# Adding the last stage's products to an output that stays in memory, by transfers that GpSimd issues

## The chip, the core and the metric

The kernel runs on one core of a Trainium2 chip. A core has five engines with instruction queues of their own: TensorE (PE in the profile; PEld are its weight loads) multiplies matrices into PSUM; VectorE (DVE), ScalarE (ACT) and GpSimd (POOL) do arithmetic; SyncE (SP) mostly issues transfers. ScalarE and GpSimd issue transfers too. All transfers run on 16 DMA engines. SBUF is the on-chip memory of 128 partitions, PSUM holds the products of TensorE, and HBM is the memory outside. In what follows, "memory" is HBM.

The metric is the device time of one execution in microseconds (us).

## What is computed

The input `u` has 2048 positions of 512 channels. Two branches are mixed by a gate, one number per position:

```python
g = sigmoid((x * gate_w).sum(-1, keepdims=True))
a = A(x)      # a long convolution per channel (state space kernel K), by FFT, plus u * Dskip
b = gelu(x @ w1 + b1) @ w2 + b2
return g * a + (1 - g) * b
```

with the convolution as

```python
K = einsum("dn,dnl,dn->dl", Cc, exp(logdA * l), dB).real
y = irfft(rfft(pad(u)) * rfft(pad(K)))[:L] + u * Dskip
```

The output is 2048 by 512 in 32-bit floats, 4 MB.

## The kernel before

The program has two parts. `front` (a list of tasks whose order a planner in the code works out from costs and due times) computes the dense branch `b`, the taps `K`, and the first stages of the Fourier transforms of signal and taps; intermediate results go to memory (`tu_d` for the signal, `tk_d` for the taps). The dense branch's result, already multiplied by `1 - g`, goes to the output tensor `out` in memory: a first half of the hidden units is stored plainly (L974), and the second half is added to it in memory by transfers that GpSimd issues with `accum_op=ALU.add` (L980), 256 KB each. Two of the 16 output tiles of the second half are left over and computed late (`late`, `rest`).

`out` is laid out as 16 tiles of 128 rows by 512 channels, and the last part handles them in eight pairs, k or m from 0 to 7; a pair is two tiles.

`conv` is the last part, and its order is written out by hand. A loop over s from 0 to 15 does, for two frequency groups at a time: `product(s)`, six VectorE instructions that multiply spectra; `signal(s + 1)` and `taps(s + 2)`, second transform stages on TensorE (L1109), whose inputs are loaded ahead by SP (L1090 from `tk_d`, and from `tu_d`); `inverse(s)`, the first stage of the inverse transform on TensorE (L1148); and `turn(s)`, in which ScalarE copies the result to SBUF (L1154) and SP stores it to `t4_d` in memory (L1156), two stores of 256 KB per step. After every eight tiles (a group) the stored rows are loaded back in another arrangement into `den` and `t3` by four transfers of 512 KB (L1164): for the first three groups GpSimd issues them, for the last one ScalarE.

In the steps from s = 8 on, `dense(s - 8)` comes last: it picks a place `mos[k]` in `attic` or `loft` (SBUF space that held the signal's transform) and SP loads pair k of `out` there (L1176), 512 KB. So pair 7's load stands in SP's queue behind the last store to `t4_d`.

After the loop `rest` finishes the two late dense tiles, four matmuls into a tile named `warm` follow (L1225; nobody reads the result), and VectorE adds the late tiles into pair 7 (L1228). Then comes the last stage, a loop over the pairs m: eight matmul instructions give two tiles in PSUM (L1236), and each is multiplied by the gate and added to the loaded dense tile. For ten of the sixteen tiles VectorE does both in one instruction (L1248). For the six in `ASIDE` ScalarE multiplies into a buffer (L1245) and GpSimd adds that (L1246). SP then stores the pair (L1252); the two tiles of pair 7 are stored singly, by SP and ScalarE (L1250).

Of the kernel before, what the change touches and what calls it, by code (L numbers as in the profile page):

```python
# [13 lines left out]
ALU = mybir.AluOpType  # L14
# [61 lines left out]
N_US = N_DEN + N_ROOM  # L76
W_DVE = ((1, 0), (3, 0), (5, 0))

ASIDE = (1, 3, 6, 8, 11, 13)
GROUP = 8  # L80

PI = float(np.pi)
# [193 lines left out]
def gated_mix(  # L276
# [18 lines left out]
    nc = tc.nc  # L295
# [778 lines left out]
    def conv(pool, ps, late, attic, loft, den):  # L1074


        sas = [pool.tile([P, D], F32, name=f"sa{k}", bufs=1) for k in range(6)]
# [5 lines left out]
        def fetch(n):  # L1083
            if n % 4 == 0:
                m = n // 4
                cc = pool.tile([P, 384], F32, tag="cc", name=f"cc{m}", bufs=4)
                nc.sync.dma_start(cc, c2[m])
                c4s[m] = cc
            t2s[n] = pool.tile([P, D], F32, tag="tk", name=f"tk{n}", bufs=N_TK)
            nc.sync.dma_start(t2s[n], tk_d[ko[n]])  # L1090

        def matrices(m):

            cc = c4s[m]
            f = cc[:, 0:256].rearrange("p (n k) -> p n k", n=4)
            f1 = pool.tile([P, 4, 64], F32, tag="f1", name=f"f1{m}", bufs=2)
            nc.scalar.mul(f1[0:64], f[64:128], -1.0)
            nc.scalar.copy(f1[64:128], f[0:64])
            mats[m] = (f, f1), cc[:, 256:384].rearrange("p (s k) -> p s k", s=2)
# [11 lines left out]
        def taps(s):  # L1111
            fac[s] = []
            for c in range(2):
                pk = ps.tile([P, D], F32, tag="pk", name=f"p2k{s}{c}", bufs=2)
                pair(s, 1, c, pk)
                k = pool.tile([P, D], F32, tag=f"k{c}", name=f"k{s}{c}", bufs=2)
                nc.scalar.copy(k, pk)  # L1117
                fac[s].append(k)

        def signal(s):  # L1120
            pus[s] = []
            for c in range(2):
                pu = ps.tile([P, D], F32, tag="pu", name=f"p2u{s}{c}", bufs=4)
                pair(s, 0, c, pu)
                pus[s].append(pu)

        def product(s):

            (ur, ui), (kr, ki) = pus.pop(s), fac.pop(s)
            v = [pool.tile([P, D], F32, tag=f"v{i}", name=f"v{s}{i}", bufs=2) for i in range(2)]  # L1130
            nc.vector.tensor_mul(v[0], ur, kr)
            nc.vector.tensor_mul(v[1], ur, ki)
            nc.vector.tensor_mul(zs[0], ui, ki)
            nc.vector.tensor_mul(zs[1], ui, kr)
            nc.vector.tensor_sub(v[0], v[0], zs[0])
            nc.vector.tensor_add(v[1], v[1], zs[1])
            prod[s] = v

        def inverse(s):

            v = prod.pop(s)
            for i in range(2):
                n = 2 * s + i
                pas[n] = ps.tile([P, D], F32, tag="pa", name=f"pa{s}{i}", bufs=2)
                r = slice(64 * i, 64 * i + 64)
                w = mats[n // 4][1][r, s % 2]
                for c in range(2):
                    nc.tensor.matmul(pas[n][64 * c : 64 * c + 64], w, v[c][r], start=True, stop=True)  # L1148

        def turn(s):  # L1150

            for n in (2 * s, 2 * s + 1):
                sa = sas[n % 6]
                nc.scalar.copy(sa, pas.pop(n))  # L1154
                g, k = divmod(n, GROUP)
                nc.sync.dma_start(t4_d[g, :, k].rearrange("e c q d -> (c q) e d"), sa)  # L1156
                if k < GROUP - 1:
                    continue
                rows = t4_d[g].rearrange("e k c q d -> (e k c) q d")

                for h in range(0, 32, 8):
                    on = nc.gpsimd if n < 31 else nc.scalar
                    to = t3[g:P:4, h - 8 : h] if h else den[g:P:4]
                    on.dma_start(to, rows[:, h : h + 8])  # L1164

        accs, mos = {}, {}

        def dense(k):

            r = 5 + 2 * k if k < 7 else 0  # L1170
            if r < N_ATTIC:
                mos[k] = attic[:, r : r + 2]
            else:
                r -= N_ATTIC
                mos[k] = loft[:, r * D : (r + 2) * D].rearrange("p (s d) -> p s d", s=2)
            nc.sync.dma_start(mos[k], out[2 * k : 2 * k + 2].rearrange("s p d -> p s d"))  # L1176

        def rest(n):

            while late and n:  # L1180
                s, h, l, w, wl = late.pop(0)
                first = s not in accs
                last = not any(e[0] == s for e in late)
                if first:
                    accs[s] = ps.tile([P, D], F32, tag="pk", name=f"acc{s}", bufs=2)
                ss = slice(s * P, (s + 1) * P)
                nc.tensor.matmul(accs[s], h[:, ss], w, start=first, stop=False)
                nc.tensor.matmul(accs[s], h[:, ss], wl, start=False, stop=False)
                nc.tensor.matmul(accs[s], l[:, ss], w, start=False, stop=last)
                n -= 1  # L1190
# [11 lines left out]
        for s in range(16):  # L1202

            for n in range(2 * s + N_TK + (2 if s else 0), min(2 * s + N_TK + 4, 32)):
                fetch(n)
            for n in range(2 * s + N_ROOM, min(2 * s + N_ROOM + 2, 32)) if s > 3 else ():
                nc.sync.dma_start(us[n], tu_d[ko[n]])
            product(s)
            if s + 1 < 16:
                signal(s + 1)  # L1210
            if s + 2 < 16:
                if s % 2 == 0:
                    matrices(s // 2 + 1)
                taps(s + 2)
            if s == 15:
                rest(N_REST)
            inverse(s)
            turn(s)
            if s >= 8:
                dense(s - 8)  # L1220
        rest(14)

        warm = ps.tile([P, D], F32, tag="pa", name="warm", bufs=2)
# [2 lines left out]
        for s in range(N_LATE):  # L1226
            z = mos[7][:, s]
            nc.vector.scalar_tensor_tensor(z, accs[s], gate[:, 1, 14 + s : 15 + s], z, ALU.mult, ALU.add)  # L1228

        for m in range(8):  # L1230
            tag, n = ("pa", 2) if m % 3 == 2 else ("pu", 4)
            pbs = [ps.tile([P, D], F32, tag=tag, name=f"pb{m}{i}", bufs=n) for i in range(2)]
            for i in range(2):
                for b in range(2):
                    j = 4 * m + 2 * i + b
                    nc.tensor.matmul(  # L1236
                        pbs[i][64 * b : 64 * b + 64], g1t[:, min(j, 1)], t3[:, j - 8] if j > 7 else den[:, j],
                        start=True, stop=True,
                    )
            for i in range(2):  # L1240
                t = 2 * m + i
                z, g = mos[m][:, i], gate[:, 0, t : t + 1]
                if t in ASIDE:
                    a = sas[ASIDE.index(t)]
                    nc.scalar.mul(a, pbs[i], g)  # L1245
                    nc.gpsimd.tensor_add(z, z, a)  # L1246
                else:
                    nc.vector.scalar_tensor_tensor(z, pbs[i], g, z, ALU.mult, ALU.add)  # L1248
                if m == 7:
                    (nc.sync, nc.scalar)[i].dma_start(out[t], z)  # L1250
            if m < 7:
                nc.sync.dma_start(out[2 * m : 2 * m + 2].rearrange("s p d -> p s d"), mos[m])  # L1252

    ctx.enter_context(tc.manual_schedule())
    keep = ctx.enter_context(tc.tile_pool(name="keep", bufs=1))
# [8 lines left out]
    with (  # L1264
        tc.tile_pool(name="fp", bufs=2, reuse_waits="tile") as fp,
        tc.tile_pool(name="ps_f", bufs=2, space=PSUM, reuse_waits="tile") as ps_f,
    ):
        conv(fp, ps_f, late, attic, loft, den)
# [64 lines left out]
```

## Time and profile before

| | us |
|---|---|
| three runs: median, lowest, highest | 539.2, 537.0, 542.56 |
| the profiled execution: time | 537.5 |
| the profiled execution: span from first to last event | 535.7 |
| `front` gives way to `conv` | about 425 |
| the last store to `t4_d` is issued | 502.7 |
| the first matmul of the last stage starts | 515.1 |
| the last matmul of the last stage ends | 530.1 |

The page of the profile gives for each engine its busy time and, in a strip of 40 slices, when it was busy; for the DMA engines the mean busy share and the rate in GB/s. The chain that ended last is followed back from the last instruction, at each step to what released it. A row of the timeline gives the start, the busy time, the engine, the line, the operation, the names of what it writes and reads, and how often it came in a row; in brackets stands the idle time before it and what ended that.

### The profile page before, as it was taken

The page shows a single profiled execution, that of the slowest core. Times are in us where ns is not written, and L with a number is a line of the kernel's source. Part 1 is how long each engine was busy: PE and PEld are TensorE (multiplying, and loading weights), DVE is VectorE, ACT ScalarE, POOL GpSimd, SP SyncE. Part 2 cuts the span into 40 slices and gives each one's busy share as a digit, 9 for nine tenths or more (in the row PEclk, how much of TensorE's full clock was granted, in tenths as well). Part 3 has the DMA queues.
Part 4 walks back from the last instruction along what each step waited for, and adds up shares of the span by engine and source line. Part 5 has one row for each costly group of instructions (what it writes and reads, how often), then busy time and mean ns, then how long its engine had stood idle before and what let it go on. Part 6 is the DMA issues. An engine that isn't in the chain of part 4 may idle for free.

```text
span 535.7 us, 12218 instructions
## 1 busy us (share of the span) xinstructions
PE 513.4 (96%) x4818; PEld 387.3 (72%) x4818; DVE 426.3 (80%) x806; ACT 353.5 (66%) x614; POOL 41.3 (8%) x79
## 2 busy tenths in 40 slices
PE   7969999999999999989999999999999999999985
PEld 6637788898899889876988988889888622222621
DVE  5798899999999959869999999999701287777233
ACT  4979956699875599966586988376342555655211
POOL 2000000000000000000112010101010101010123
PEclk9779999999999999999999999999999999999999
DMA  8989674153585442583878037705778858999976
GB/s 260 347 287 308 196 253 138 41 199 90 133 233 171 158 123 78 167 268 76 212 173 258 2 88 145 162 6 133 233 185 181 239 184 272 368 406 373 356 292 260
DMA packets 82469, 107.87 MB, mean 201 GB/s; under 512 B 39318, under 2 KB 43546, under 8 KB 81900
## 3 DMA queue, kind: packets, MB, share of 16 engines
q1 hardware_dynamic: 77020, 86.09, 50.2%
q0 software_dynamic: 5056, 18.65, 13.2%
q10 hardware_dynamic: 336, 2.36, 1.2%
q8 instruction: 38, 0.62, 0.5%
q14 instruction: 19, 0.16, 0.1%
HBM read 61.46 MB, written 45.62 MB: 200 GB/s over the span
## 4 chain that ended last, share of the span: by engine, by line
PE 74%; DMA 11%; ACT 9%; DVE 2%; issue 2%; SPq 0%; ACTq 0%; DVEq 0%
PE pk L682 10%; PE ph L900 8%; PE acc L948 8%; PE ph L902 8%; PE ph L901 8%; PE acc L950 7%; PE acc L949 7%; PE p2u L1109 6%; PE p2k L1109 5%; PE pa L1148 3%; PE pb L1236 3%; DMA attic<-in_xs_dram 2%; DMA tu_d<-attic 2%; PE ph L404 2%; DMA t_d<-sa 2%
## 5 line engine op out<-in xcount | busy, mean ns | idle before, releaser
L900 PE MATMUL ph<-xh,wh 128*128 128x256 f32 x448 | 129.2, 288 | 4.2 <-ACT attic L422 2.3
L902 PE MATMUL ph<-xh,wl 128*128 128x256 f32 x448 | 128.2, 286 | 0.5 <-DVE wl L783 0.4
L901 PE MATMUL ph<-xlo,wh 128*128 128x256 f32 x448 | 127.8, 285 | 0.0
L900 PEld LDWEIGHTS ph<-xh,wh 128*128 128x128 f32 x448 | 86.2, 192 | 14.7 <-issue 5.6
L948 PE MATMUL acc<-wh,hh 128*128 128x512 f32 x210 | 85.5, 407 | 3.0 <-ACT hh L920 3.0
L901 PEld LDWEIGHTS ph<-xlo,wh 128*128 128x128 f32 x448 | 86.3, 193 | 2.0
L902 PEld LDWEIGHTS ph<-xh,wl 128*128 128x128 f32 x448 | 86.4, 193 | 1.2 <-DVE wl L783 1.2
L950 PE MATMUL acc<-wh,hl 128*128 128x512 f32 x210 | 83.3, 396 | 0.4 <-DVE hl L930 0.4
L949 PE MATMUL acc<-wl,hh 128*128 128x512 f32 x210 | 83.2, 396 | 0.0
L917 ACT ACTIVATE ph<-ph,b1t 128x256 f32<-128x256 f32 x112 | 50.4, 450 | 43.1 <-PE ph L902 41.1
L930 DVE TENSOR_TENSOR hl<-ph,hh 128x512 fp32r<-128x512 f32 (+1 forms) x62 | 38.2, 617 | 31.8 <-ACT hh L920 31.5
L682 PE MATMUL pk<-y,den 128*32 128x64 f32 x2048 | 61.4, 290 | 0.0
L682 PEld LDWEIGHTS pk<-y,den 128*32 128x32 f32 x2048 | 57.2, 136 | 3.7 <-issue 1.4
L948 PEld LDWEIGHTS acc<-wh,hh 128*128 128x128 f32 x210 | 40.0, 191 | 18.0 <-issue 6.8
L950 PEld LDWEIGHTS acc<-wh,hl 128*128 128x128 f32 x210 | 39.8, 190 | 10.7 <-DVE hl L930 1.7
L644 DVE TENSOR_TENSOR y<-y,ea 128x64 f32<-128x64 f32 (+4 forms) x80 | 45.2, 565 | 0.2
L949 PEld LDWEIGHTS acc<-wl,hh 128*128 128x128 f32 x210 | 40.0, 191 | 6.8
L920 ACT CAST hh<-ph 128x512 fp32r<-128x512 f32 (+1 forms) x62 | 33.0, 533 | 10.3 <-PE acc L949 6.9
L489 DVE TENSOR_TENSOR loft<-den,zz 128x256 f32<-128x256 f32 (+2 forms) x48 | 37.2, 775 | 1.6 <-ACT den L615 1.2
L490 DVE TENSOR_TENSOR loft<-den,zz 128x256 f32<-128x256 f32 (+2 forms) x48 | 37.1, 773 | 0.0
L657 DVE TENSOR_TENSOR y<-y,loft 128x2048 f32<-128x2048 f32 x16 | 36.5, 2283 | 0.0
L1117 ACT COPY k<-p2k 128x512 f32<-128x512 f32 x32 | 18.8, 586 | 25.8 <-issue 14.8
(175 smaller groups left out, 876.2 us busy)
## 6 DMA issues: line engine op xcount, KB each, us to landing
tu_d<-attic SPq DMA_DIRECT2D x64, 128.0 KB, 3.3
tk_d<-sk SPq DMA_DIRECT2D x32, 256.0 KB, 5.0
tk<-tk_d SPq DMA_DIRECT2D x32, 256.0 KB, 4.2
t_d<-sa SPq DMA_DIRECT2D x32, 256.0 KB, 5.8
t<-t_d POOLq DMA_DIRECT2D x9, 512.0 KB, 7.6
attic<-in_xt_dram SPq DMA_DIRECT2D x16, 256.0 KB, 4.1
xh_d<-xh SPq DMA_DIRECT2D x8, 512.0 KB, 3.7
xl_d<-xlo SPq DMA_DIRECT2D x8, 512.0 KB, 4.5
```

What stands on the lines that cost most here:

```text
L489: vec(2 * m, lambda: vv.tensor_mul(t, a, br), due, [ka, *kb], [kt])
L644: nc.vector.tensor_mul(both(n, 64 - 3 * n, n), both(0, 64 - n, n), an)
L682: nc.tensor.matmul(pks[q][32 * j : 32 * j + 32, :, gg], x[:, r, :, ch], y[:, r, :, ch], start=(r == 0), stop=(r == 1), skip_group_check=True,)
L900: nc.tensor.matmul(p, h, xh[xk][:, d], start=(d == 0), stop=False)
L901: nc.tensor.matmul(p, h, xlo[xk][:, d], start=False, stop=False)
L902: nc.tensor.matmul(p, lo, xh[xk][:, d], start=False, stop=(d == 3))
L917: nc.scalar.activation(phs[q][:, n], phs[q][:, n], AF.Gelu_apprx_tanh, bias=b1t[:, f : f + 1])
L930: nc.vector.tensor_sub(lo, phs[q][:, 0:nf], hi.bitcast(F32))
L948: nc.tensor.matmul(a, h, wh[1][w], start=start, stop=False)
L949: nc.tensor.matmul(a, h, wl[1][w], start=False, stop=False)
L950: nc.tensor.matmul(a, l, wh[1][w], start=False, stop=(j == 3))
L1109: nc.tensor.matmul(out[64 * i : 64 * i + 64], w, x, start=True, stop=True)
```

## The change

Six of the eight pairs (0 to 5) of the dense output are no longer loaded. `room` gives each pair its place in SBUF, as `dense` did, without the load. In the last stage the gated product alone is written there: for the first tile of a pair by VectorE (`tensor_scalar`), for the second by ScalarE. GpSimd then issues one transfer per pair, 512 KB, that adds the product to `out` in memory. Pairs 6 and 7 are still loaded, now after steps 12 and 13 of the loop instead of steps 14 and 15, and VectorE multiplies and adds all four of their tiles; they are stored plainly as before. The six GpSimd additions and the list `ASIDE` go. (The loads at steps 8 to 11 are gone; `rest`, the `warm` matmuls and L1228 stay.)

```diff
-ASIDE = (1, 3, 6, 8, 11, 13)
 GROUP = 8
@@
-        def dense(k):
+        def room(k):
 
             r = 5 + 2 * k if k < 7 else 0
             if r < N_ATTIC:
@@
                 mos[k] = loft[:, r * D : (r + 2) * D].rearrange("p (s d) -> p s d", s=2)
-            nc.sync.dma_start(mos[k], out[2 * k : 2 * k + 2].rearrange("s p d -> p s d"))
@@
             inverse(s)
             turn(s)
-            if s >= 8:
-                dense(s - 8)
+            if 12 <= s < 14:
+                k = s - 6
+                room(k)
+                nc.sync.dma_start(mos[k], out[2 * k : 2 * k + 2].rearrange("s p d -> p s d"))
         rest(14)
@@
+            if m < 6:
+                room(m)
             for i in range(2):
                 t = 2 * m + i
                 z, g = mos[m][:, i], gate[:, 0, t : t + 1]
-                if t in ASIDE:
-                    a = sas[ASIDE.index(t)]
-                    nc.scalar.mul(a, pbs[i], g)
-                    nc.gpsimd.tensor_add(z, z, a)
+                if m > 5:
+                    nc.vector.scalar_tensor_tensor(z, pbs[i], g, z, ALU.mult, ALU.add)
+                elif i:
+                    nc.scalar.mul(z, pbs[i], g)
                 else:
-                    nc.vector.scalar_tensor_tensor(z, pbs[i], g, z, ALU.mult, ALU.add)
+                    nc.vector.tensor_scalar(z, pbs[i], g, None, ALU.mult)
                 if m == 7:
                     (nc.sync, nc.scalar)[i].dma_start(out[t], z)
-            if m < 7:
-                nc.sync.dma_start(out[2 * m : 2 * m + 2].rearrange("s p d -> p s d"), mos[m])
+            to = out[2 * m : 2 * m + 2].rearrange("s p d -> p s d")
+            if m < 6:
+                nc.gpsimd.dma_start(to, mos[m], accum_op=ALU.add)
+            elif m < 7:
+                nc.sync.dma_start(to, mos[m])
```

## The prediction

> **What bounds the kernel now.** I read the page's head first, then the stages in time (the table of busy time per stretch), then the chain that ended last, and only then the single instructions of the tail.
>
> ```profile
> span 535.7 us, 12218 instructions
> PE 513.4 (96%) x4818; PEld 387.3 (72%) x4818; DVE 426.3 (80%) x806; ACT 353.5 (66%) x614; POOL 41.3 (8%) x79
> ```
>
> TensorE is busy for 96% of the span, but the change touches only the last 65 us, so the stage's own rows decide. The columns of the next table that matter are the last two: share of the 16 DMA engines that is busy, and GB/s.
>
> ```profile
> 366.90:370.60 3.70, 3.70 (x66) 3.57 (x68) 2.79 (x6) 2.43 (x4) 0.33 (x1) 1.00 0.98 142
> 398.20:402.20 4.00, 4.00 (x35) 4.00 (x36) 0.54 (x1) 3.37 (x7) 0.30 (x1) 1.00 0.98 143
> 420.90:424.90 4.00, 3.84 (x28) 2.83 (x26) 1.61 (x3) 2.55 (x7) 0.00 (x0) 1.00 1.10 245
> 473.00:496.00 23.00, 22.93 (x118) 6.28 (x116) 17.88 (x30) 12.56 (x24) 2.08 (x5) 1.00 1.03 388
> 497.00:511.00 14.00, 14.00 (x65) 8.85 (x64) 2.98 (x5) 2.15 (x4) 0.98 (x2) 1.00 1.01 367
> 519.00:530.00 11.00, 10.16 (x48) 3.21 (x44) 5.21 (x7) 3.27 (x5) 6.05 (x6) 1.00 0.67 251
> ```
>
> From 473 to 511 the DMA engines are full (1.03 and 1.01) with plain transfers, at 388 and 367 GB/s. The first two rows are two places where almost nothing moves but a pair of accumulating stores of the dense output: the engines are as full (0.98), and move 142 GB/s. The third row has such a pair among plain transfers. The chain that ended last then shows where the full DMA reaches the end:
>
> ```profile
> 487.01 0.07 issue
> 487.09 2.46 PE p2k L1109 x8
> ...
> 492.44 1.72 PE p2k L1109 x8
> ...
> 502.68 8.27 DMA t_d<-sa
> ...
> 511.12 3.82 DMA den<-t_d
> 514.94 0.14 issue
> 515.08 7.10 PE pb L1236 x32
> 522.18 0.03 issue
> 522.21 0.76 DVE loft L1248
> 522.97 0.04 issue
> 523.01 7.11 PE pb L1236 x32
> 530.12 0.03 issue
> 530.15 0.75 DVE attic L1248
> ```
>
> TensorE runs on without gaps, except for about 0.8 us at 487 (0.07, and 2.46 where the same step takes 1.72) spent on a late load. The last store of the inverse transform to `t4_d` then takes 8.27 us, its reload 3.82, the last 64 matmuls 15.04 (515.08 to 530.12) and what follows them 5.6 (to 535.7).
>
> **The change, part by part.** *Six loads go, two move.* A pair is 512 KB, as the first row below has it, or 0.524 MB; at 388 GB/s it takes 1.35 us of all 16 engines, so six loads are 8.1 us taken out of the full stretch. Of the eight loads seven stood ahead of the last store in SP's queue; now two do (pairs 6 and 7, at steps 12 and 13). That is five times 1.35, 6.75 us of work less ahead of it.
>
> ```profile
> attic<-out_dram SPq DMA_DIRECT2D x4, 512.0 KB, 8.9
> t<-t_d POOLq DMA_DIRECT2D x9, 512.0 KB, 7.6
> t_d<-sa SPq DMA_DIRECT2D x32, 256.0 KB, 5.8
> DMA to landing us min/median/max: 2.4/5.8/11.5
> ```
>
> Stores to `t4_d` (the third row, and the spread of their times to landing under it) take 2.4 us at best; the last has 8.27, so some 5.9 us is queue, a little less than what goes. The reload of the third group (four transfers of 512 KB, 2.1 MB, 5.4 us at 388 GB/s) stays in the stretch, and it too starts earlier. I take a landing 4.6 us after an issue at 501.9 (0.8 us earlier than 502.68, the late load at 487 being gone): 506.5, with 504.3 and 510.1 as ends. Pair 7's load is moved past the stores of steps 14 and 15 in SP's queue, and pair 6's past those of steps 13 and 14: they add their 2.7 us there, counted above. Their targets were last read by matmuls that stand ahead in TensorE's order, so no wait is added.
>
> *What is late next.* Behind the transform stand four matmuls whose results nobody reads.
>
> ```profile
> 509.00 3.65 PE L1225 MATMUL warm<-z,cc 128*64 128x512 f32 x8
> 518.54 3.63 PE L1236 MATMUL pb<-t,g1t 128*64 128x512 f32 x16
> 523.01 7.09 PE L1236 MATMUL pb<-t,g1t 128*64 128x512 f32 x32 [0.84 <-DVE loft L1248]
> ```
>
> They end at 512.65; the next may start 0.19 before that (as 518.54 stands before 515.08 plus 3.65), and all moves up by 0.8: the last stage starts at 511.7 instead of 515.08, 3.4 us earlier, if the reload is there, that is, if the store has landed by 507.7 (less 3.82 and 0.17 between 510.95 and 511.12). At 506.5 it has; at the worst end, 510.1, the start would be 514.1. The rest of the gain in the queue is lost to TensorE's own work.
>
> *VectorE, ScalarE, GpSimd arithmetic.* VectorE keeps ten instructions in the stage, ScalarE six, now in alternation, and GpSimd loses six additions.
>
> ```profile
> 517.12 0.69 ACT L1245 ACTIVATE sa<-pb,gate 128x512 f32<-128x512 f32 x1 [14.59 <-DMA t<-t_d]
> 517.89 1.27 POOL L1246 TENSOR_TENSOR attic<-attic,sa 128x512 f32<-128x512 f32 x1 [19.90 <-ACT sa L1245]
> ```
>
> A pair's products take two matmul tiles (1.72 us of TensorE) and 0.69 and about 0.75 us on two engines, so the engines stay hidden, and the 0.84 us stall before 523.01 may go. The sixteen products would end at 525.9. Pair 0's second product is ready where the old one was, 2.7 us after the stage's start (517.12 plus 0.69), and each pair comes 1.72 later.
>
> *Six accumulating stores in place of six plain ones.* This is the dear part. What the trace has are pairs of such stores of 256 KB:
>
> ```profile
> 365.47 1.76 POOL L980 DMA_DIRECT2D out_dram<-io  x2 [4.29 <-ACT io L969]
> DMA  0100000000194998899959249999984000003000
> L980 POOL DMA_DIRECT2D out_dram<-io x14: 848/959/1215, 267.6 to 417.6; - x14
> out_dram<-io POOLq DMA_DIRECT2D x2, 256.0 KB, 4.3
> ```
>
> The second line cuts 365 to 372 into 40 slices: the engines start about 1.45 us after the issue at 365.47 and are full until about 370.6. So 512 KB in two stores costs 0.524 MB at 142 GB/s, 3.69 us. In the mixed row, 245 GB/s over 4 us is 0.98 MB; less the pair's 0.524, at 388 GB/s the plain part is 1.17 us, and 2.83 us is left for the pair. The two ends are 2.83 and 3.69. A store of 512 KB has one start where the pair has two, and the last two of the six run beside plain stores; I take 3.3 for four and 2.83 for two, 18.9 us in all, nearer to the lone pairs in what is alone. GpSimd spends 0.85 to 1.22 us to issue one store of 128 rows; one of 256 rows is at most 2.43, less than the transfer that it starts, so issuing delays only the first. For the first data I take 1.9 us after the issue (1.45 at least, 2.9 at most). GpSimd has nothing else queued behind these waits, and eight completion slots serve six stores.
>
> Pairs 6 and 7 still go out by plain stores, 1.05 MB, 2.7 us at 388 GB/s. They share the engines with the queue of accumulating ones. The Trainium skill, DMA: Bandwidth & Descriptors, section "Issuing engines are not separate DMA queues", says that transfers issued by any engine run on the same 16 DMA engines and interleave; the mixed row agrees, with 1.10 of busy share. By that rule the 2.7 us is added, as done here; without it the sum would be 2.7 us shorter.
>
> *The sum.* Start of the stage 511.7; first data 2.7 plus 1.9 later; 18.9 of accumulating; 2.7 of plain stores; 0.3 to the receipt, and 1.4 from the last landing to the end of the span, read here:
>
> ```profile
> 530.93 0.40 ACTq L1250 DMA_DIRECT2D out_dram<-attic  x1
> out_dram<-attic ACTq DMA_DIRECT2D x1, 256.0 KB, 3.4
> ```
>
> (530.93 plus 3.4 is 534.3, the span ends at 535.7.) That is 511.7 + 4.6 + 18.9 + 2.7 + 1.7 = 539.6, a span 3.9 us longer. The profiled execution took 537.5 us for its span of 535.7, so 541.4 for its like; it lies 1.7 below the median of the three runs (539.2, from 537.0 to 542.56), so I forecast 543.0 as a median. The bill: 3.4 us earlier at the start, and 7.3 us more from there to the end, because after TensorE is done the accumulating queue is still about half full.
>
> **Rivals.** *Faster: accumulating costs no more than a plain store.* With 1.35 us each the stores keep pace with TensorE and the old tail sets the end: 535.7 less 515.08 is 20.6, less the stall of 0.84, from 511.7: 531.5, or 4.2 us less, 535.0 as a median. It needs all six done in 18.4 us from the stage's start, so (18.4 - 4.6 - 2.7)/6, 1.85 us each. For it speaks only that the store is the same size; against it stand 142 and 143 GB/s at a full 0.98. The Trainium skill, the same page, section "Anatomy of one DMA — SWDGE (gpsimd) path", gives 2.0 us plus bytes over 436 GB/s for a transfer issued by GpSimd, which for 512 KB is 1.2 us behind the fixed part and would make this rival true; the two rows disagree, for the accumulating kind.
>
> *Slower by more than 1%: the queue runs at the rate of the lone pairs throughout.* Six times 3.69 is 22.1 in place of 18.9, 3.2 us more: a span of 542.8 and 546.2 as a median. It decides from 5.4 us over before, that is 20.4 us for the six, 3.4 each. For it: both lone rows; against it: one start in place of two, and the mixed row.
>
> *The stage does not start earlier.* If the reload of the third group and the two moved loads keep the last store's queue as long as it was, the start is 514.1 to 515.1, and the tail's 7.3 us stays: 2.4 to 3.4 more than the forecast, 545.4 to 546.4. Against it: 6.75 us of work less, and 4 us between the forecast landing and the old one.
>
> **How the numbers follow.** About 1%, 5.4 us, is what a measurement of this kernel can tell from no change. Forecast, as summed: 0.50. Lone-pair rate throughout or worse: 0.30. No earlier start: 0.07. Cheap accumulation: 0.13. The forecast's own range, with six stores between 17.0 and 20.4 us and the first data between 1.45 and 2.9, is 540.7 to 545.5. To hold 8 in 10 the range reaches up over the slower rival with the late first data and slow start (546.2 plus 1.0 plus 1.8, 549), and down to 536, half-way into what lies between the forecast's bottom and the cheap case, whose 535.0 is left out. Slower by over 1%: the slower rival's 0.30, the late start's 0.07, and little of the forecast: 0.38. Faster by over 1% needs more than the cheap case gives: 0.06. Within 1%: 0.56.
>
> **What would show it.** The p2k step at 487 back to 1.72 us; the last `t4_d` store at 4 to 5 us instead of 8.27; the first pb matmul at about 511.7 right behind the warm ones; DMA share near 1.0 at some 140 to 180 GB/s from 516 to 538, with TensorE done by about 526; the chain ending in a store from attic or loft issued by GpSimd. I am wrong if the last thing to land is pair 7's plain store, if these stores move over 285 GB/s, if they don't spread over all 16 engines (then many times dearer), or if the pb stage starts where it did.

## The result: half a per cent slower

Over 22 runs each, the changed kernel took 540.98 us (median; 538.26 to 544.97) and the kernel before 537.82 us (535.64 to 543.01). The ratio is 1.005, with a 95% interval from 1.0028 to 1.0071: 3 us slower, where 3.8 us had been forecast (543.0 against 539.2) and a change within 1% was held likeliest. Of the 2.0 us by which the median lies under the forecast, 1.4 come from the kernel before, whose median is 539.2 in the three runs known then and 537.82 in 22. The profiled execution has a span of 539.9 us; the forecast's sum gave 539.6.

The same stretches of the table of busy time, for the profile after (last two columns: DMA share, GB/s). The first is the queue of adding stores alone, the second the same queue with the plain stores of pairs 6 and 7 in it:

```profile
518.50:527.50 9.00, 7.29 (x32) 2.01 (x31) 3.43 (x5) 2.09 (x4) 4.68 (x4) 1.00 1.12 195
527.50:537.30 9.80, 1.24 (x6) 0.14 (x2) 1.82 (x3) 0.00 (x0) 0.01 (x1) 0.69 1.01 239
```

The DMA engines are full from 518 to 537, at 195 GB/s as long as only adding stores are there. In the second row TensorE has almost nothing left to do. The profile before had 0.67 and 251 GB/s in its tail: the engines had time to spare.

The chain that ended last in the profile after, from the first step of the hand-ordered part on; it ends in arithmetic, since it is followed through instructions and the last wait is one for transfers:

```profile
426.34 1.08 PE p2k L1108 x4
...
487.81 1.72 PE p2k L1108 x8
...
509.06 3.15 PE warm L1225 x7
512.21 0.06 PE pb L1236
512.26 0.37 PE warm L1225
512.63 6.87 PE pb L1236 x31
519.50 1.10 PE pb L1236 x4
520.63 0.76 DVE loft L1250
521.44 1.96 PE pb L1236 x8
523.42 0.76 DVE loft L1250
524.23 4.54 PE pb L1236 x20
528.79 0.75 DVE attic L1246
```

The late load at 487 is gone (1.72, it was 2.46), the 8.27 us of the last store is no longer in the chain, and the last stage follows on the `warm` matmuls at 512.2, as the prediction had it (511.7); in the timeline its first matmul runs from 511.6, beside the last two of them. From there TensorE needs until 528.8. The end, 11 us later, is in the transfers that GpSimd issues:

```profile
515.40 1.23 POOL L1255 DMA_DIRECT2D out_dram<-attic  x1 [22.31 <-ACT attic L1248]
...
526.34 1.17 POOL L1255 DMA_DIRECT2D out_dram<-loft  x1 [1.61 <-ACT loft L1248]
```

GpSimd issues the first at 515.4 and the sixth at 526.3, 1.2 us for each. Their times to landing grow from 5.8 us for the first to 10.6 for the last (the rows give the size of a transfer and the median time to landing in us):

```profile
out_dram<-attic POOLq DMA_DIRECT2D x3, 512.0 KB, 7.9
out_dram<-loft POOLq DMA_DIRECT2D x3, 512.0 KB, 9.2
out_dram<-loft SPq DMA_DIRECT2D x1, 512.0 KB, 9.3
out_dram<-attic SPq DMA_DIRECT2D x1, 256.0 KB, 8.9
```

The last two rows are plain stores. Pair 6's too takes 9.3 us, where such stores took 3.1 us in the profile before. The other, a tile of pair 7, is issued at 528.7 and is the last of all to land, at 537.6; the last adding store lands at 536.9. And behind the last landing stands one more thing, in the instructions that close the program (count, shortest/median/longest duration in ns, first and last start):

```profile
L1331 POOLq DRAIN  x3: 51/93/12836, 526.3 to 539.7; - x3
L1331 SPq DRAIN  x3: 7/7/7, 537.7 to 539.4; - x3
```

SP, which waits for every transfer, has seen all of them land at 537.7; GpSimd's drain, begun at 526.3, lasts 12.8 us, to 539.15, and only then the engines meet for the end.

### The profile page after: what moved, and what is told of

Its sections match the earlier page's. It is cut to its first block, busy times and chain, and to the rows that moved or that the text cites. A ratio compares the mean times of both kernels' runs of the same rounds, so it can differ in the third digit from the quotient of the medians.

```text
span 539.9 us, 12181 instructions
## 1 busy us (share of the span) xinstructions
PE 511.7 (95%) x4818; PEld 385.6 (71%) x4818; DVE 426.8 (79%) x806; ACT 353.5 (65%) x614; POOL 40.9 (8%) x79
## 4 chain that ended last, share of the span: by engine, by line
PE 76%; DMA 9%; ACT 8%; DVE 3%; issue 1%; SPq 1%; ACTq 0%; DVEq 0%
PE pk L681 10%; PE ph L899 8%; PE acc L947 8%; PE ph L901 8%; PE ph L900 8%; PE acc L949 7%; PE acc L948 7%; PE p2u L1108 5%; PE p2k L1108 5%; PE pa L1147 3%; PE pb L1236 3%; DMA tu_d<-attic 3%; DMA attic<-in_xs_dram 2%; PE ph L403 2%; ACT L916 1%
## 5 line engine op out<-in xcount | busy, mean ns | idle before, releaser
L900 PEld LDWEIGHTS ph<-xlo,wh 128*128 128x128 f32 x448 | 85.9, 192 | 2.0
```

The source lines that it names most:

```text
L900: nc.tensor.matmul(p, h, xlo[xk][:, d], start=False, stop=False)
```

## The experiments

All times from a profile vary with where the planned first part ends: the first step of the hand-ordered part (426.34 above, 425.55 before) lies between 423.6 and 427.4 in the twelve profiles, with the same code ahead of it (but for the order of the output's rows in the kernel with 4 KB rows). So the table counts from that step, in us, one profile for each kernel; the ratios to the kernel before come from the repeated runs.

| kernel | ratio [95% interval] | from that step to the last stage | to the end |
|---|---|---|---|
| before | 1 | 89.5 | 110.2 |
| changed: 6 pairs added in memory | 1.005 [1.0028, 1.0071] | 85.9 | 113.6 |
| 6 plain stores by GpSimd, dense part left out | 0.9909 [0.9877, 0.9941] | 86.8 | 107.9 |
| 6 plain stores by SP, dense part left out | 0.9932 [0.9902, 0.9962] | 87.7 | 108.5 |
| 4 pairs added | one run, 536.73 us | 87.2 | 111.3 |
| 3 pairs added | 0.9973 [0.994, 1.0005] | 87.4 | 110.1 |
| 2 pairs added | 0.9992 [0.9963, 1.0021] | 88.2 | 109.9 |
| 1 pair added | 0.9985 [0.9962, 1.0008] | 88.4 | 108.7 |
| before, loads two steps earlier | 0.9969 [0.9942, 0.9997] | 89.3 | 110.0 |
| the same, all tiles on VectorE | 0.9963 [0.9939, 0.9988] | 88.9 | 107.2 |
| changed, 4 KB rows | 1.0051 [1.0021, 1.0081] | 86.8 | 113.4 |
| changed, 2 `warm` matmuls | 1.0079 [1.0046, 1.0111] | 86.8 | 115.4 |

### Plain stores in place of the adding ones

```diff
-                nc.gpsimd.dma_start(to, mos[m], accum_op=ALU.add)
+                nc.gpsimd.dma_start(to, mos[m])        # first kernel
+                nc.sync.dma_start(to, mos[m])          # second kernel
```

> The six transfers are issued by GpSimd as in the changed kernel, but store the products plainly, so pairs 0 to 5 of the output lack the dense part. Theory 'price of accumulating' (an accumulating store of 512 KB holds the DMA engines for some 3.1 us, a plain one for 1.35): the queue empties with TensorE, the end is set by pair 7's stores after a stage that starts at 512.4 us; a span of about 534 us, 1.5 to 2 us under the kernel before, DMA rate of 300 GB/s and more where it was 200. Rival 'GpSimd' (what costs is that GpSimd issues them, and its drain at the end, 1.5 us behind the last landing in the changed kernel): a span of 538 us or more.

> The products of pairs 0 to 5 are stored plainly by SP, the dense part of them is left out; so this has the loads gone and nothing dearer at the end. Theory: a stage start at 512.4 us and a span of 533.5 to 534.5, equal to the plain GpSimd stores within 0.5 us; this is all that taking six loads away is worth (1.5 to 2 us), less than the 3.4 us that the prediction put on it, since the two stalls of TensorE of 0.85 us each stay. Rival 'GpSimd': 3 us or more faster than the GpSimd stores.

Measured: spans of 532.9 and 532.7 us, about 1 us less than expected, and ratios of 0.9909 and 0.9932. So adding is what costs. With GpSimd issuing the same six transfers of the same size and only the adding taken away, the end came 5.7 us earlier (107.9 for 113.6 from the first step). Who issues makes no difference beyond the intervals. Against the kernel before, the ratios make the missing loads worth 4.9 and 3.7 us, the table only 2.2 and 1.7; the rest would lie ahead of the first step, where the code is the same, and is not explained. The DMA engines in the profile of the plain stores by GpSimd, over the whole tail:

```profile
515.00:531.00 16.00, 11.32 (x50) 3.24 (x46) 6.31 (x9) 3.44 (x5) 4.00 (x6) 1.00 0.69 263
```

At 0.69 they have slack again, and move more (263 GB/s; 300 and more had been expected) than when they were full with adding stores (195). GpSimd's drain does no harm here: its last transfer lands before SP's do, and the drain is over in time.

### Fewer pairs added in memory

Three, four, two and one pair; the others are loaded as soon as their place is free (step k + 6), and VectorE multiplies and adds them. In each kernel the number stands in place of N.

```diff
-            if 12 <= s < 14:
+            if N + 6 <= s < 14:       # N = 3, 4, 2, 1
@@
-            if m < 6:                 # room(m), and the adding transfer
+            if m < N:
@@
-                if m > 5:
+                if m >= N:
```

> Three pairs (0 to 2) are added in memory, five are loaded (at steps 9 to 13). Theory: three accumulating stores need 9.3 us from 517 and are done at about 526 to 527, before TensorE is; the end is set by pair 7; if the stage starts at 512.4 to 513, a span of 533.5 to 534.5, ratio 0.996 to 0.998. Rival 'GpSimd drain' (a fixed cost for accumulating at all): 536 or more. Rival 'five loads keep the queue long': a stage start of 514.5 or later and a span of 535 to 537.

> Four pairs are added in memory. Theory 'work of the tail': between the three pairs (535.4) and the six (539.9), 1.5 us per pair: 536.5 to 537.5, its last landing from GpSimd followed by a drain of 2.1 us. Rival 'fixed cost of accumulating': near one of the two, not between.

> Two pairs are added in memory, six are loaded (steps 8 to 13). Theory 'work of the tail': the DMA engines have 2.9 us for each accumulating store and 1.35 for each plain pair after about 517, so 2 x 2.9 + 6 x 1.35 = 13.9, done at 531, at the same time as what TensorE's end (528) lets pair 7 do; a span of 532.5 to 534, ratio 0.992 to 0.996, the best of 0, 2, 3 and 6 pairs. Rival 'start': with six loads the last store is as late as with eight, and the kernel equals the one with the loads merely moved (534.4).

> One pair is added in memory, seven are loaded (steps 7 to 13). Theory 'work of the tail': 2.9 + 7 x 1.35 = 12.4 us of DMA from 517 on, done at 529.5, before pair 7's stores could be (TensorE's end at 528 plus 3.5), so the dear store costs nothing and one load less stands in the queue: equal to or up to 0.5 us better than all sixteen tiles on VectorE with no adding in memory, ratio 0.992 to 0.996. Rival 'any adding in memory costs at the end': 1 us or more slower than that.

From the first step to the end: 113.6, 111.3, 110.1, 109.9 and 108.7 us for six, four, three, two and one pair, and 107.2 with none (the kernel with all tiles on VectorE, told of further down). That is about 1 us a pair, in uneven steps of 0.2 to 1.6, so a smaller fixed cost beside it is not excluded. It is a balance. Each pair less brings a load back, and the last stage starts later; but from its start to the end it takes 27.7 us with six pairs, then 24.2, 22.7, 21.8, 20.3, and 18.3 with none, 1.6 us a pair.

The expectations missed on both sides. Four pairs ended sooner than expected (a span of 535.0 for 536.5 to 537.5). Three pairs were to give 0.996 to 0.998, and 0.9973 is there, but by its interval it can't be told from no change; its span of 535.4 is above the 534.5 expected. With two pairs the span was 537.4 for the 532.5 to 534 expected, in part because this profile's first step came at 427.44, but the ratio of 0.9992 misses 0.992 to 0.996 as well. Counted from the first step, this kernel ends with the one whose loads are merely moved (109.9 and 110.0), as its rival had it, though its last store lands 1.5 us earlier. With one pair the dear store was to cost nothing. The rival was nearer, by which any adding costs 1 us or more at the end: in this profile 6.3 us passed from TensorE's end to the end of the span (528.1 to 534.4), with no pair added 4.3 (526.6 to 530.9).

The tail of both in the table of busy time, first the kernel with one pair added, then the one without any adding (told of further down):

```profile
515.00:532.00 17.00, 13.09 (x62) 4.99 (x58) 11.27 (x15) 0.69 (x1) 1.23 (x1) 0.96 0.91 295
```

```profile
515.00:532.00 17.00, 11.58 (x54) 4.32 (x50) 10.87 (x15) 0.00 (x0) 0.00 (x0) 0.92 0.70 267
```

A share of 0.91 with one adding store, 0.70 with none. The trace's packet records show where the time went. The adding store's packets run from 518.9 to 522.7. SP issued the first plain store at 518.6, but its first packet starts at 522.3, 3.7 us later; with nothing added that took 0.9 us. From there plain packets keep the engines full to 532. So the work that I had put (2.9 us for the adding store and 1.35 for each of seven plain pairs) was nearly right, except that the adding store took 3.8; but it begins at 518.9 and not at 517, and so it ends behind TensorE. The two ratios overlap (0.9985 and 0.9963).

### The loads moved, nothing added in memory

```diff
-            if s >= 8:
-                dense(s - 8)
+            if 6 <= s < 14:
+                dense(s - 6)
```

> The kernel before, with all eight loads two steps earlier (steps 6 to 13) and nothing else changed. Theory 'queue': what matters is how much stands ahead of the last store in a full stretch; the bytes are the same, but two steps (9.2 us) of it move to where the DMA engines were not quite full, so the last store takes 5.5 to 7.5 us and the stage starts at 513 to 514.5, a span 0.5 to 2 us shorter. Rival 'place' (the two loads just ahead of the last stores make the wait): the last store at 4.5 us and a start of 512.4, a span of 533. Rival 'bytes alone': no change, 515 and 535.7.

The second kernel has besides this:

```diff
-ASIDE = (1, 3, 6, 8, 11, 13)
+ASIDE = ()
```

> The kernel before with the loads two steps earlier, and VectorE multiplying and adding all sixteen tiles (no ScalarE and GpSimd in the stage). Nothing is added in memory. In the kernel with two pairs added VectorE did fourteen tiles and TensorE ran 64 matmuls in 14.2 us without a stall. Theory 'work of the tail': eight plain stores are 10.8 us of DMA, no bound, so the stall of 0.85 us goes and the end moves with TensorE: 0.8 us less than with the loads merely moved, ratio 0.993 to 0.997 to the kernel before. Rival: VectorE at 0.75 us a tile falls behind TensorE's 0.86; no gain over the loads merely moved (0.997).

Moving the loads makes the last store's wait shorter, but an earlier load comes later. The chain of the first of the two kernels:

```profile
476.04 11.08 DMA tk<-tk_d
...
487.26 2.48 PE p2k L1109 x8
...
502.86 6.65 DMA t_d<-sa
509.61 4.05 DMA den<-t_d
513.79 7.10 PE pb L1236 x32
```

The store takes 6.65 us (8.27 before; 5.5 to 7.5 expected). But three of the moved loads now stand ahead of the `tk` load at 476.04, where one stood before. In the profile before, that load is in this row:

```profile
474.84 1.76 SPq L1090 DMA_DIRECT2D tk<-tk_d  x2
```

It took no less there (12.1 us for 11.08), but it was issued 49.3 us after the first step, and is now at 51.6. TensorE waits longer for it, and the last store is issued 78.4 us after the first step instead of 77.1. Of the 1.6 us won, 0.2 is left at the start of the last stage. The ratio, 0.9969, is lower than these 0.2 us account for, and that is not explained. The bytes did not go away, and the stretch that they moved into is as full: the profile before has 1.00 there.

```profile
455.00:473.00 18.00, 18.00 (x96) 4.93 (x94) 14.33 (x24) 10.62 (x20) 0.55 (x2) 1.00 1.00 374
```

I had expected slack in that stretch; there was none. The second kernel's chain has the last stage in one piece:

```profile
512.63 13.97 PE pb L1236 x64
```

13.97 us for the 64 matmuls, where two halves and a stall took 15.04. Its ratio is 0.9963 with an interval from 0.9939 to 0.9988, and its end, 107.2 us after the first step, is the earliest of the twelve profiles (by the ratios the kernels of plain stores, which leave work out, are still ahead). It is faster than the kernel before and, by the intervals, than the changed one. From the loads merely moved (0.9969) the ratio can't tell it, so the gain from the missing stall is shown by the profiles alone.

### Rows of 4 KB, and fewer idle matmuls

The output's rows are put in another order in memory, and back in order when the result is read out, so that a partition's two rows of a pair are one row of 4 KB:

```diff
+    wide = out.rearrange("(m i) p d -> m (i p d)", i=2).rearrange("m (p e) -> m p e", p=P)
...
-            to = out[2 * m : 2 * m + 2].rearrange("s p d -> p s d")
+            to, mo = wide[m], mos[m].rearrange("p s d -> p (s d)")
...
-                nc.gpsimd.dma_start(to, mos[m], accum_op=ALU.add)
+                nc.gpsimd.dma_start(to, mo, accum_op=ALU.add)
```

> The changed kernel with another order of rows in memory: the two rows of a pair that one SBUF partition holds lie next to each other, so that each row of an accumulating store is 4 KB and not 2 KB. Theory 'per byte' (the adding itself is slow, 178 ns for 2 KB on one engine): packets of some 340 ns, the same rate of 180 to 200 GB/s, a span of 539 to 540. Rival 'per packet' (a fixed time to read and write back, whatever the size): packets under 240 ns, 280 GB/s and more, and a span of 534 to 536.

The price goes by the byte. In the trace's packet records an adding packet took 178 ns for 2 KB and 328 ns for 4 KB (medians), and the rate is the same (193 GB/s for 195). Plain packets took 84 ns for 2 KB, and 169 ns for 4 KB in the plain stores by GpSimd. So size for size adding takes about twice as long, and the larger packets of those plain stores are not what made them cheap. The row of the kernel with 4 KB rows:

```profile
519.50:528.50 9.00, 7.29 (x34) 2.05 (x32) 3.00 (x4) 2.52 (x4) 3.27 (x4) 1.00 1.05 193
```

The other kernel of this pair:

```diff
-N_KEEP = 4
+N_KEEP = 2
```

> The changed kernel with two in place of four matmuls into the tile that nobody reads. The prediction held that these matmuls, not the reload, set the start of the last stage once the queue is short. Theory: the start moves from right behind them to the landing of the reload, 0.5 to 1.2 us earlier counted from the first step of the last part, and the end with it, since the accumulating queue starts as much earlier: a span of about 539. Rival: the reload sets it already; no change within 0.3 us.

Neither theory had this. The stage starts 86.8 us after the first step, where the changed kernel has 85.9, and the end comes 1.8 us later; by the ratios (1.0079 and 1.005) the intervals of the two overlap. The column before the last two is the clock granted to TensorE:

```profile
509.00:513.00 4.00, 1.75 (x6) 0.50 (x6) 0.48 (x1) 0.00 (x0) 0.00 (x0) 1.00 0.87 287
513.00:516.00 3.00, 3.00 (x12) 1.13 (x10) 0.75 (x1) 0.69 (x1) 0.00 (x0) 0.68 0.77 306
516.00:520.00 4.00, 4.00 (x18) 1.47 (x16) 1.50 (x2) 0.78 (x2) 2.05 (x2) 0.81 0.54 67
```

And its chain at that place:

```profile
512.67 0.14 issue
512.80 9.87 PE pb L1236 x36
```

TensorE was idle for 2.25 us before 512.80, and from 513 to 520 it was granted 0.68 and 0.81 of its clock (half of it from 514.1 to 517.5); the first 36 matmuls took 9.87 us where they took 8.18 in the kernels of plain stores. But the length of the gap alone can't be the cause. The kernel before idles for 2.44 us at the same place, and its clock stays at 1.00 there and behind it:

```profile
515.08 3.65 PE L1236 MATMUL pb<-den,g1t 128*64 128x512 f32 x16 [2.44 <-DMA den<-t_d]
512.50:519.40 6.90, 4.46 (x22) 1.78 (x23) 2.77 (x4) 1.26 (x2) 1.27 (x1) 1.00 0.82 293
```

What sets the two gaps apart was not tested. So it stays open whether two of the four idle matmuls could go.

## Why the prediction came out right

*Six loads go, two move.* The step at 487 is back to 1.72. Counted from the first step, the last store is issued 0.8 us earlier (76.3 for 77.1), as forecast; in the clock of the page it is not (502.68 in both), since this profile's first part ended 0.8 us later. The last store landed 4.5 us after its issue (4.6 forecast). That was luck of this profile: in the four others with the same two loads (both kernels of plain stores, 4 KB rows, two `warm` matmuls) it took 5.7 to 6.3 us. The queue ahead of it became shorter than the 8.27 us of before, but not by as much as forecast.

*What is late next.* The stage starts 3.7 us earlier counted from the first step (3.4 forecast), and 1.8 to 2.8 us earlier in those four. That TensorE's `warm` matmuls set it is true of this one profile, by a hair: in the profiles of plain stores, of fewer pairs and of 4 KB rows the chain comes to the stage through the store and the reload, 0.9 to 2.6 us later than here. The step should have said that both are late at about the same time.

*VectorE, ScalarE, GpSimd.* The stall of 0.85 us that "may go" became two of them (521.44 and 524.23 in the chain), and TensorE ended at 528.8, not 525.9. It cost nothing here, because the queue of stores set the end; with plain stores the same two stalls are in the chain. The kernel with all tiles on VectorE has none. Why they come was not looked into.

*Six adding stores.* This is the term that decided, with the sign forecast, and its size was too high. At 195 GB/s a store of 0.524 MB takes 2.7 us, 0.6 less than the 3.3 that I took for stores that stand alone, and below the lower end of 2.83. The lone pairs of the kernel before kept the engines as busy (0.98) and have the same median packet of 178 ns; but their slow packets, of 300 ns and more, bring the mean to 224 ns, against 187 in the queue. Why they are slow is not known. The first data came 1.8 us after the first issue (1.9 forecast). From the first issue to the last landing it was 22.2 us (515.4 to 537.6) against 23.8 in the sum (1.9, 18.9, 2.7 and 0.3).

*The end.* From the last landing to the end of the span I took 1.4 us, as read from plain stores. It was 2.3, since GpSimd's drain ended 1.4 us after SP had seen everything land. So the sum met the span within 0.3 us because errors cancel: the stage's start 0.5 us late (512.2 for 511.7, with a first part that ended 0.8 us later in this profile), the first issue 3.2 us behind it instead of 2.7, the stores 1.6 us shorter, the end 0.9 us longer.

*The signs.* The step at 487, the full engines and the early start came as named; the rate was 195 GB/s and more, above the 140 to 180 named. One sign of being wrong came up: pair 7's plain store was the last thing to land, 0.7 us behind the last adding store. It does not speak for cheap adding, since that store took 8.9 us behind the queue, against 2.9 with plain stores throughout; and what ended the program was still GpSimd's drain behind the adding stores. But the sign was badly chosen, since it can't tell a slow queue from a fast one when both kinds of store share the engines.

*The rivals.* Cheap adding is refuted by the plain stores, 0.9909 against 1.005. Its own sum, 4.2 us less than before, is about what the plain stores gave (4.9 and 3.7). The formula of the Trainium skill (DMA: Bandwidth & Descriptors, "Anatomy of one DMA — SWDGE (gpsimd) path"), under which this rival would have come true, does not hold for adding transfers: 2.7 us each in a full queue, where it has 1.2 us behind the fixed part. For the plain stores by GpSimd it does: medians of 3.3 and 3.2 us from issue to landing, where 2.0 and 1.2 make 3.2. The queue at the rate of the lone pairs throughout, and the stage that starts no earlier, did not come about either.

## What to carry to other kernels

Adding in memory by a transfer saves a load, but this case's trace has it at about half the rate of a plain store and by the byte (178 ns for a packet of 2 KB, 84 for a plain one), so I would count it as two stores. Before using it, ask whether the DMA engines have that time free where it falls. Here they had not: six loads left a full stretch, and their price came back, and more, in the tail; even one pair ended no sooner than none. A queue's price is read from a stretch in which the queue is full; single transfers overstate it. Work that is taken off one full stretch and put into another one ends on the next wait, as the moved loads did.

## What was not expected of the hardware

The drain with which GpSimd closes the program ends 2.0 to 2.2 us after the last landing of GpSimd's own transfers, in the ten profiles where a transfer is the last that GpSimd does; in the changed kernel it ended 1.4 us behind everybody else. In the other two, the kernel before among them, GpSimd's last work is an addition, and the drain ended 3.9 us after it. An idle stretch of 2.25 us before the last stage was followed by 3.4 us at half of TensorE's clock, 1.7 us on 36 matmuls, while one of 2.44 us in the kernel before was not; what decides is open. A plain store that SP issues beside an adding one starts late: its first packet came 3.7 us after the issue with one pair added and 3.5 us in the changed kernel, where it is 0.9 us with none.
